# A fused retention and gated feed-forward kernel: loading the first weight slice ahead of the second pair's q and v, and splitting the first block of x in two

## The chip, the cores and the metric

The kernel runs on one core of a Trainium2 chip. The metric is the device time of one execution in microseconds (us); smaller is better. Engines are named as in the profile: PE is TensorE's matmul, PEld its weight load, DVE VectorE, ACT ScalarE, POOL GpSimd, SP SyncE.

## What is computed

There are 4 sequences of 768 tokens with 8 heads of 64 channels. The first half of the work is a retention recurrence, the second a feed-forward block with a sigmoid gate over all 3072 tokens, with a model width of 512 and a hidden width of 1536:

```python
# retention: q, k, v are [4, 8, 768, 64]; gamma = 1 - 2 ** (-5 - h)
for t in range(S):
    state = gamma * state + k[t] outer v[t]
    y[t] = scale * (q[t] @ state)
# feed-forward: x is y with the heads side by side, [3072, 512]
out = (sigmoid(x @ w_gate) * (x @ w_val)) @ w_out
```

## The kernel before

**Retention in chunks.** The recurrence is worked off in 24 chunks of 128 tokens. A chunk needs the transposes of k and q (PE, then a copy out of the accumulator by ACT or DVE), the scores of k against q (PE), a causal mask on them (DVE), the product of q with the state so far (`inter`), the product of the masked scores with v (`intra`), the chunk's own addition to the state (`state`, summed by DVE and cast by ACT), and a multiplication by a decay table that leaves the chunk's 128 columns of x (`y_out`, DVE). The first four chunks have versions of their own, whose names end in `_run`: chunks 0 and 1 are the first pair, 2 and 3 the second, and each pair's k, q and v come in one load (`kr`, `qr`, `vr`, line 75). `scale_run` (line 265) multiplies v by a table, and both `state_run` and `intra_run` need its result.

**Feed-forward in blocks of 512 tokens.** There are six such blocks, t = 0 to 5. An "up" (`up`, line 364) is one of the 12 slices of 128 hidden channels, n1: four matmuls with `wg`, four with `wv`, a sigmoid on ACT and a product on DVE that writes `hT`. `up_columns` (line 378) does the same for two values of n1 on 256 of the 512 tokens. A "down" multiplies `hT` by `wo` for 128 tokens and writes rows of the output. The first block of x is made by the first four chunks, so that its ups can begin only when `y_out_run` has delivered columns.

**Order.** The order of the instructions of each engine is the order in which the Python text issues them; nothing is rearranged. Each engine works its own list in order and waits on semaphores where an operand comes from another engine. Lines 435 to 508 write the start out by hand; after that, a table `plan` says behind which up or down of a block a step of the retention is put. Loads that convert to bf16, and most others, are issued by POOL one after the other (lines 98 to 109, 437, 445, 451, 452, 480 to 487), so POOL's own operations stand in the same list as its loads. Before the change, that list is: k of the first pair, q of the first pair, k, q and v of the second pair, a mask, gate and value slice 0, another mask, slices 1 and 2, the second `scale_run`, a decay table, slices 3 to 5, two more tables, four slices of `wo`, and the chunks from 4 on. A gate and value slice s (line 84) serves the ups n1 = 2s and 2s + 1.

**Identity products.** `keep_on(n)` (line 411) issues n matmuls of the identity with itself whose result nobody reads. They stand in PE's list at five places of the start, 29, 5, 9, 10 and 24 of them, each 128 columns wide.

The start of PE's list is, in order: 29 identity products; transposes of k, `state_run(0)`; 5 identity products; transposes of q; 9 identity products; `scores_run(0)`; transposes of the second pair's k; `inter_run`; transposes of the second pair's q; `intra_run(0)`; 10 identity products; `scores_run(1)`; `inter_run(2)`; 24 identity products; `state_run(1)`; up n1 = 0 on the first 256 tokens; `inter_run(3)`; `intra_run(1)`; ups 1 to 3 on the first 256 tokens; ups 0 to 3 on the second 256 tokens; then ups 4 to 11 on 512 tokens each.

Of the kernel before, what the change touches and what calls it, by code (L numbers as in the profile page):

```python
# [9 lines left out]
F32 = mybir.dt.float32  # L10
BF16 = mybir.dt.bfloat16
I32 = mybir.dt.int32
AX = mybir.ActivationFunctionType
ALU = mybir.AluOpType
# [3 lines left out]
def kernel(  # L18
# [10 lines left out]
    nc = tc.nc  # L29
# [3 lines left out]
    C = 128  # L33
# [41 lines left out]
    def load_run(x, a, dtype, eng, name):  # L75
        t = const.tile([128, H, 2 * D], dtype, name=name, tag=name, bufs=1)
        eng.dma_start(out=t, in_=x[0, :, a * 2 * C:(a + 1) * 2 * C, :].rearrange("h (p j) d -> p h (j d)", j=2))
        return t
# [5 lines left out]
    def load_gate_val(s):  # L84
        cols = slice(s * 256, (s + 1) * 256)
        for dst, w in ((wg, moe_w_gate), (wv, moe_w_val)):
            nc.gpsimd.dma_start(out=dst[:, :, cols],  # L87
                                in_=w.rearrange("(kk p) n -> p kk n", p=128)[:, :, cols])
# [9 lines left out]
    kr[0] = load_run(k, 0, BF16, nc.gpsimd, "kr0")  # L98
    ident = const.tile([128, 128], BF16, name="ident")
    make_identity(nc, ident)  # L100
    tokr = const.tile([128, 2, 2], I32, name="tokr")
    nc.gpsimd.iota(tokr, pattern=[[2 * C, 2], [1, 2]], base=0, channel_multiplier=2)
    tokv = const.tile([128, NCH], I32, name="tokv")
# [2 lines left out]
    toky = const.tile([128, 384], I32, name="toky")  # L106
    nc.gpsimd.iota(toky, pattern=[[1, 384]], base=0, channel_multiplier=0)
    kr[1] = load_run(k, 1, BF16, nc.gpsimd, "kr1")
    qr[1] = load_run(q, 1, BF16, nc.gpsimd, "qr1")

    lgh = const.tile([128, H], F32, name="lgh")
    for h in range(H):
# [23 lines left out]
    def tab_y(c):  # L136
        first = c if c in taby else c - 1
        return taby[first][:, :, (c - first) * C:(c - first + 1) * C]

    def make_taby(c, pairs=range(NP)):  # L140
        n = taby[c].shape[2]
        for p in pairs:
            nc.scalar.activation(taby[c][:, p, :], toky[:, c * C:c * C + n], AX.Exp, scale=lgp[:, p:p + 1], bias=lsc)
# [8 lines left out]
    def bank(shape, dt=F32):  # L152
        return pf.tile(shape, dt, tag="ff", name="ff")
# [50 lines left out]
    def state_out(g, z):  # L204
        for i in range(2):
            half = slice(i * D, (i + 1) * D)
            nc.scalar.copy(zbd[g % 4][half, :, half], z[half])  # L207
# [20 lines left out]
    def intra(g):  # L228
        first = g % NCH == 0
        for p in range(NP):  # L230
            for i, st in enumerate((stA[g], stB[g])):
                nc.tensor.matmul(y[g][i * D:(i + 1) * D, p, :], vs[g][:, 2 * p + i, :], st[:, p, :],  # L232
                                 start=(first and p == 0), stop=True, skip_group_check=True)

    def y_out(g):
        c = g % NCH
        if g % 4 == 0:
            xT[g // 4] = at.tile([128, NP, 512], BF16, tag="xT", name="xT")
        col = (g % 4) * C
        nc.vector.tensor_tensor(xT[g // 4][:, :, col:col + C], y[g], tab_y(c), op=ALU.mult)  # L240


    kT, qT = {}, {}
# [21 lines left out]
    def scale_run(a, eng):  # L265
        vsr[a] = const.tile([128, H, 2, D], BF16, name=f"vsr{a}")
        eng.tensor_tensor(vsr[a], runs(vr[a]), tabr[:, a].unsqueeze(3).to_broadcast([128, H, 2, D]), op=ALU.mult)  # L267
# [54 lines left out]
        else:  # L322
            nc.vector.tensor_tensor(new_za(g), za[g - 1], zz[g], op=ALU.add)

    def y_out_run(g):
        if g == 0:
            xT[0] = at.tile([128, NP, 512], BF16, tag="xT", name="xT")
        cols = slice(g * C, (g + 1) * C)
        in_runs = "x n (p j) -> x n j p"
        nc.vector.tensor_tensor(xT[0][:, :, cols].rearrange(in_runs, j=2), y[g].rearrange("x n (j p) -> x n j p", j=2),  # L330
                                tab_y(g).rearrange(in_runs, j=2), op=ALU.mult)

    def step_t(g):
        transposes(g)
# [27 lines left out]
    hT = {}  # L362

    def up(t, n1, lo=0, hi=512):
        if t not in hT:
            hT[t] = ffn.tile([128, NFF, 512], BF16, tag="hT", name="hT", bufs=2)
        ps = []
        for w in (wg, wv):
            u = bank([128, 512])
            for kk in range(KT):  # L370
                nc.tensor.matmul(u[:, lo:hi], w[:, kk, n1 * 128:(n1 + 1) * 128], xT[t][:, kk, lo:hi],  # L371
                                 start=(kk == 0), stop=(kk == KT - 1))
            ps.append(u)
        gs = ffn.tile([128, 512], F32, tag="gs", name="gs")
        nc.scalar.activation(gs[:, lo:hi], ps[0][:, lo:hi], AX.Sigmoid)  # L375
        nc.vector.tensor_tensor(hT[t][:, n1, lo:hi], gs[:, lo:hi], ps[1][:, lo:hi], op=ALU.mult)  # L376

    def up_columns(t, n1s, lo, hi):
        n = hi - lo
        ps = []  # L380
        for w in (wg, wv):
            u = bank([128, 512])
            for i, n1 in enumerate(n1s):
                for kk in range(KT):
                    nc.tensor.matmul(u[:, i * n:(i + 1) * n], w[:, kk, n1 * 128:(n1 + 1) * 128], xT[t][:, kk, lo:hi],  # L385
                                     start=(kk == 0), stop=(kk == KT - 1))
            ps.append(u[:, :len(n1s) * n])
        gs = ffn.tile([128, 512], F32, tag="gs", name="gs")
        g = gs[:, :len(n1s) * n]
        nc.scalar.activation(g, ps[0], AX.Sigmoid)  # L390
        nc.vector.tensor_tensor(hT[t][:, n1s[0]:n1s[-1] + 1, lo:hi], g.rearrange("p (i n) -> p i n", n=n),  # L391
                                ps[1].rearrange("p (i n) -> p i n", n=n), op=ALU.mult)
# [15 lines left out]
        row = t * 512 + sm * 128  # L408
        nc.sync.dma_start(out=out[row:row + 128, :], in_=ob)

    def keep_on(n, u=None):
        if u is None:
            u = bank([128, 512])
        for _ in range(n):
            nc.tensor.matmul(u[:, :128], ident, ident, start=True, stop=True)  # L415

    def last_down(t):
        row = t * 512 + 384
# [15 lines left out]

    make_taby(0)
    scale_run(0, nc.vector)
    vr[1] = load_run(v, 1, F32, nc.gpsimd, "vr")
    maskr = const.tile([128, 2, 2, D], F32, name="maskr")
    nc.gpsimd.memset(maskr, 1.0)
    for i in range(2):  # L440
# [1 line left out]
        nc.gpsimd.affine_select(half, half, pattern=[[-1, 2], [1, 2], [2, D]], base=0, channel_multiplier=-2,  # L442
                                compare_op=ALU.is_ge, fill=0.0)
    maskr2 = maskr.rearrange("x j i p -> x (j i p)").unsqueeze(1).to_broadcast([128, 2, 4 * D])
    load_gate_val(0)
    causal = const.tile([128, 128], F32, name="causal")
    nc.gpsimd.memset(causal, 1.0)
    nc.gpsimd.affine_select(causal, causal, pattern=[[1, 128]], base=0, channel_multiplier=-1,
# [1 line left out]
    causal4 = causal.unsqueeze(1).to_broadcast([128, NP, 128])  # L450
    load_gate_val(1)
    load_gate_val(2)
    scale_run(1, nc.gpsimd)
    make_taby(2, range(2))
    warm = bank([128, 512])
    keep_on(29, warm)
    kT[0], qT[0], kT[1], qT[1] = (new_run_T() for _ in range(4))
    transpose_run(kr[0], kT[0], [nc.scalar])
    state_run(0)
    sum_run(0)  # L460
    sum_run(1)
    keep_on(5, warm)
    transpose_run(qr[0], qT[0], [nc.scalar, nc.vector])
    state_out(0, zz[0])
    state_out(1, za[1])
    keep_on(9, warm)
    scores_run(0)
    masks_run(0, 0)
    masks_run(0, 1)
    transpose_run(kr[1], kT[1], [nc.scalar])  # L470
    make_taby(2, range(2, 4))
    inter_run(0)
    inter_run(1)
    transpose_run(qr[1], qT[1], [nc.scalar])
    nc.scalar.preload_act_table(AX.Sigmoid)
    intra_run(0)
    y_out_run(0)
    y_out_run(1)
    extend_taby(3)
    for s in range(3, NFF // 2):  # L480
        load_gate_val(s)
# [3 lines left out]
        load_out(s)  # L485
    for g in range(4, 8):
        load_chunk(g)
    keep_on(10)
    scores_run(1)
    masks_run(1, 0)  # L490
    inter_run(2)
    keep_on(24)
    state_run(1)
    sum_run(2)
    state_out(2, za[2])
    masks_run(1, 1)
    sum_run(3)
    up(0, 0, 0, 256)
    inter_run(3)
    intra_run(1)  # L500
    y_out_run(2)
    y_out_run(3)
    up(0, 1, 0, 256)
    state_out(3, za[3])
    up(0, 2, 0, 256)
    up(0, 3, 0, 256)
    up_columns(0, range(0, 2), 256, 512)
    up_columns(0, range(2, 4), 256, 512)


    def ups(t):
# [2 lines left out]
    def downs(t):  # L514
        return [lambda sm=sm, i=i: down(t, sm, i) for sm in range(4) for i in range(2)]

    plan = {
        0: [(9, step_t, 4), (11, step_t, 5), (12, block, None, 4), (12, casts, 4), (13, step_t, 6), (14, block, 4, None)],
        1: [(0, step_t, 7), (2, block, None, 6), (3, step_t, 8), (4, casts, 6), (5, step_t, 9), (7, block, 6, 8),
            (9, casts, 8), (11, step_t, 10), (13, step_t, 11), (15, block, 8, 10), (17, casts, 10), (20, block, 10, None),  # L520
            (22, scale_v, 12), (23, scale_v, 13)],
# [7 lines left out]
    for t in range(NT):  # L529
        groups = ups(t) + downs(t)  # L530
        if t == NT - 1:
            groups[-2:] = [lambda: last_down(t)]
        if t == 0:
            groups = groups[4:]
            for g in range(8, 12):
                load_chunk(g)
        if t == 1:
            groups[:10] = [lambda n1=n1: up(1, n1, 0, 256) for n1 in range(10)]
            groups[10:10] = [lambda n1=n1: up_columns(1, range(n1, n1 + 2), 256, 512) for n1 in range(0, 10, 2)]
            for g in range(12, 16):  # L540
                load_chunk(g)
        if t == 2:
            load_chunk(18)
            load_chunk(19)
        if t == 3:
            load_chunk(22)
            load_chunk(23)
        for i, group in enumerate(groups):
            if i == len(groups) - 9:
                for g in range(4 * t + 8, 4 * t + 12):  # L550
                    if XBAR <= g < NG:
                        xbar(g)
            if t == 1 and i == len(groups) - 4:
                load_chunk(16)
                load_chunk(17)
            if t == 2 and i == len(groups) - 4:
                load_chunk(20)
                load_chunk(21)
            group()
            for at_group, step, *g in plan[t]:  # L560
                if at_group == i:
                    step(*g)
# [30 lines left out]
```

## Time and profile before

| | |
|---|---|
| median of 13 runs | 237.13 us |
| lowest and highest of them | 235.15 and 238.11 us |
| the execution that was profiled | 237.16 us |
| its span, in which the profile's times count | 235.5 us |
| PE busy | 224.4 us, 95% of the span |
| DVE, ACT, POOL busy | 118.3, 90.8, 77.2 us |
| moved by DMA | 27.05 MB |

The 13 runs fall in two groups: five lie between 235.15 and 235.76 us, eight between 236.92 and 238.11 us. The profiled execution belongs to the second group and is close to the median.

The profile is one execution. Its span runs from the first to the last instruction; the 1.66 us between span and time lie around it. A line of the timeline gives the start in us, the duration of the group in us, the engine, the line of the kernel, the operation, the result and its operands, shapes and the count; in square brackets stands for how long the engine was idle just before and what released it. "issue" there means that the profile shows no operand for which the engine waited. PEclk is the clock that was granted to PE, as a share of the full one.

### The profile page before, as it was taken

The page shows a single profiled execution, that of the slowest core. Times are in us where ns is not written, and L with a number is a line of the kernel's source. Part 1 is how long each engine was busy: PE and PEld are TensorE (multiplying, and loading weights), DVE is VectorE, ACT ScalarE, POOL GpSimd, SP SyncE. Part 2 cuts the span into 40 slices and gives each one's busy share as a digit, 9 for nine tenths or more (in the row PEclk, how much of TensorE's full clock was granted, in tenths as well). Part 3 has the DMA queues.
Part 4 walks back from the last instruction along what each step waited for, and adds up shares of the span by engine and source line. Part 5 has one row for each costly group of instructions (what it writes and reads, how often), then busy time and mean ns, then how long its engine had stood idle before and what let it go on. Part 6 is the DMA issues. An engine that isn't in the chain of part 4 may idle for free.

```text
span 235.5 us, 4687 instructions
## 1 busy us (share of the span) xinstructions
PE 224.4 (95%) x1904; PEld 128.2 (54%) x1925; DVE 118.3 (50%) x226; ACT 90.8 (39%) x167; POOL 77.2 (33%) x99
## 2 busy tenths in 40 slices
PE   4996999999999999999999999999999999999994
PEld 4773844456889745454545445445445454444444
DVE  5665343436887474185952546845256712234301
ACT  5953333344656421444340432621632421333211
POOL 7899856998852453426000000000000000000000
PEclk9997999999999999999999999999999999999999
DMA  8999999999999999989702253002200001200022
GB/s 138 218 185 196 200 206 210 220 235 246 230 152 101 154 171 229 202 142 161 89 0 90 93 109 70 0 0 92 90 0 3 0 32 66 85 0 0 1 92 89
DMA packets 73302, 27.05 MB, mean 115 GB/s; under 512 B 59840, under 2 KB 68928, under 8 KB 73280
## 3 DMA queue, kind: packets, MB, share of 16 engines
q0 software_dynamic: 55440, 16.78, 66.6%
q1 hardware_dynamic: 17696, 9.90, 17.8%
q8 instruction: 15, 0.25, 0.4%
q10 hardware_dynamic: 144, 0.07, 0.1%
q14 instruction: 7, 0.06, 0.1%
HBM read 28.31 MB, written 6.29 MB: 147 GB/s over the span
## 4 chain that ended last, share of the span: by engine, by line
PE 77%; DMA 10%; POOL 6%; DVE 2%; issue 2%; ACT 1%; DVEq 0%
PE ff L371 39%; PE ff L402 24%; DMA wv<-in_moe_w_val_dram 4%; DMA kn<-in_k_dram 4%; PE ff L385 4%; PE ff L232 2%; PE ff L183 2%; DMA vr<-in_v_dram 2%; POOL wg L87 2%; POOL wv L87 2%; PE ff L195 2%; PE ff L162 1%; PE ff L423 1%; PE z L201 1%; POOL vsr L267 1%
## 5 line engine op out<-in xcount | busy, mean ns | idle before, releaser
L376 DVE TENSOR_TENSOR hT<-gs,ff 128x512 bf16<-128x512 f32 (+1 forms) x72 | 45.2, 634 | 63.9 <-PE ff L371 58.9
L371 PE MATMUL ff<-xT,wg 128*128 128x512 bf16 (+1 forms) x277 | 68.1, 361 | 1.2 <-DVE xT L330 0.7
L371 PE MATMUL ff<-xT,wv 128*128 128x512 bf16 (+1 forms) x287 | 68.5, 362 | 0.1
L375 ACT ACTIVATE gs<-ff 128x512 f32<-128x512 f32 (+1 forms) x72 | 39.9, 556 | 71.8 <-PE ff L371 64.7
L402 PE MATMUL ff<-wo,hT 128*128 128x512 bf16 x267 | 61.1, 379 | 0.9 <-issue 0.5
L371 PEld LDWEIGHTS <-wv 128*128 128x128 bf16 x288 | 28.6, 99 | 28.5
L402 PEld LDWEIGHTS <-hT 128*128 128x128 bf16 x276 | 26.3, 98 | 31.2 <-DVE hT L376 0.6
L371 PEld LDWEIGHTS <-wg 128*128 128x128 bf16 x288 | 27.4, 99 | 28.3 <-issue 0.8
L407 ACT COPY ob<-ff 128x512 f32<-128x512 f32 x23 | 13.5, 586 | 49.1 <-PE ff L402 40.2
L62 POOL DMA_DIRECT2D vf<-in_v_dram x20 | 18.3, 917 | 17.5 <-DVE vs L174 10.5
L240 DVE TENSOR_TENSOR xT<-ff,taby 128x512 bf16<-128x512 f32 x20 | 12.9, 686 | 21.0 <-PE ff L232 21.0
L67 POOL DMA_DIRECT2D kn<-in_k_dram x20 | 18.1, 905 | 13.4 <-DMA qkX<-kn 7.3
L207 ACT CAST zbd<-za 64x256 bf16<-64x256 f32 x38 | 15.3, 403 | 11.0 <-DVE za L219 8.0
L68 POOL DMA_DIRECT2D qn<-in_q_dram x20 | 18.2, 908 | 1.9 <-DMA wo<-in_moe_w_out_dram 1.6
L188 DVE TENSOR_TENSOR stA<-ff,causal 128x512 bf16<-128x512 f32 x20 | 13.6, 681 | 0.0
L189 DVE TENSOR_TENSOR stB<-ff,causal 128x512 bf16<-128x512 f32 x20 | 13.6, 681 | 0.0
L174 DVE TENSOR_TENSOR vs<-vf,tabv 128x512 bf16<-128x512 f32 x20 | 13.4, 684 | 0.0
L415 PE MATMUL ff<-ident 128*128 128x128 bf16 x77 | 6.6, 255 | 3.0 <-POOL ident masks.py:199 3.0
L164 ACT ACTIVATE qkT<-ff 128x1024 bf16<-128x1024 bf16 x8 | 8.2, 1026 | 1.6 <-PE ff L162 1.6
L391 DVE TENSOR_TENSOR hT<-gs,ff 128x512 bf16<-128x512 f32 x7 | 4.7, 687 | 5.5 <-PE ff L385 4.3
L415 PEld LDWEIGHTS <-ident 128*128 128x128 bf16 x77 | 5.7, 117 | 3.2 <-POOL ident masks.py:199 3.0
L385 PE MATMUL ff<-xT,wg 128*128 128x256 bf16 x56 | 7.3, 273 | 0.0
(85 smaller groups left out, 159.4 us busy)
## 6 DMA issues: line engine op xcount, KB each, us to landing
out_dram<-ob SPq DMA_DIRECT2D x23, 256.0 KB, 2.2
vf<-in_v_dram POOLq DMA_DIRECT2D x20, 256.0 KB, 6.8
kn<-in_k_dram POOLq DMA_DIRECT2D x20, 128.0 KB, 7.2
qn<-in_q_dram POOLq DMA_DIRECT2D x20, 128.0 KB, 7.6
wg<-in_moe_w_gate_dram POOLq DMA_DIRECT2D x6, 256.0 KB, 7.3
wv<-in_moe_w_val_dram POOLq DMA_DIRECT2D x6, 256.0 KB, 7.8
wo<-in_moe_w_out_dram POOLq DMA_DIRECT2D x4, 384.0 KB, 10.6
vr<-in_v_dram SPq DMA_DIRECT2D x1, 512.0 KB, 4.3
```

The source lines that it names most:

```text
L62: nc.gpsimd.dma_start(out=vf[g], in_=src(v, g))
L67: nc.gpsimd.dma_start(out=kn[g], in_=src(k, g))
L68: nc.gpsimd.dma_start(out=qn[g], in_=src(q, g))
L188: nc.vector.tensor_tensor(stA[g], sc[g][0], causal4, op=ALU.mult)
L189: nc.vector.tensor_tensor(stB[g], sc[g][1], causal4, op=ALU.mult)
L207: nc.scalar.copy(zbd[g % 4][half, :, half], z[half])
L371: nc.tensor.matmul(u[:, lo:hi], w[:, kk, n1 * 128:(n1 + 1) * 128], xT[t][:, kk, lo:hi], start=(kk == 0), stop=(kk == KT - 1))
L375: nc.scalar.activation(gs[:, lo:hi], ps[0][:, lo:hi], AX.Sigmoid)
L376: nc.vector.tensor_tensor(hT[t][:, n1, lo:hi], gs[:, lo:hi], ps[1][:, lo:hi], op=ALU.mult)
L385: nc.tensor.matmul(u[:, i * n:(i + 1) * n], w[:, kk, n1 * 128:(n1 + 1) * 128], xT[t][:, kk, lo:hi], start=(kk == 0), stop=(kk == KT - 1))
L402: nc.tensor.matmul(o, hT[t][:, n1, sm * 128:(sm + 1) * 128], wo[:, n1, :], start=(n1 == 0), stop=(n1 == NFF - 1))
L407: nc.scalar.copy(ob, o)
```

## The change

- Gate and value slice 0 takes the place of the second pair's q in POOL's list. The second pair's v and q come behind the first mask, v before q.
- The scaling of the second pair's v moves from POOL to DVE, behind the first pair's `y_out_run`.
- A block of x is held as two parts of 256 tokens, `[128, 2, NP, 256]`, instead of `[128, NP, 512]`. The first pair's `y_out_run` is done in halves: first channels 0 to 255 of both chunks, then the rest.
- Identity products are 512 columns wide (the identity is read four times over) and are 8, 2, 2, 4 and 2 in number. They all write the tile `warm`.
- The second pair's q is transposed behind the first ups instead of before `intra_run(0)`, and its copy is shared by ACT and DVE.
- Ups 0 to 5 (not 0 to 3) are done on 256 tokens at a time with `up_columns`. The first two come right behind the first pair, in two rows: the products with channels 0 to 255 of x, then the rest. Ups 2 and 3 on the first part stand between `inter_run(2)` and `inter_run(3)`, ups 4 and 5 behind `intra_run(1)`; the second part follows for all six. The table `plan` for block 0 is shifted by two, so each of its steps stands behind the same up or down as before.
- `state_run(1)` comes before `scores_run(1)`, and `sum_run(3)` between the two calls of `masks_run(1, ...)`. The load of the sigmoid's table on ACT comes before the first `inter_run`.

The core of the diff:

```diff
     kr[1] = load_run(k, 1, BF16, nc.gpsimd, "kr1")
-    qr[1] = load_run(q, 1, BF16, nc.gpsimd, "qr1")
+    load_gate_val(0)
...
-            xT[g // 4] = at.tile([128, NP, 512], BF16, tag="xT", name="xT")
+            xT[g // 4] = new_xT()
...
-    def up_columns(t, n1s, lo, hi):
+    def up_columns(t, n1s, lo, hi, rows=1):
         n = hi - lo
-        ps = []
-        for w in (wg, wv):
-            u = bank([128, 512])
-            for i, n1 in enumerate(n1s):
-                for kk in range(KT):
-                    nc.tensor.matmul(u[:, i * n:(i + 1) * n], w[:, kk, n1 * 128:(n1 + 1) * 128], xT[t][:, kk, lo:hi],
-                                     start=(kk == 0), stop=(kk == KT - 1))
+        us = [bank([128, 512]), bank([128, 512])]
+        for row in range(rows):
+            for w, u in zip((wg, wv), us):
+                for i, n1 in enumerate(n1s):
+                    for kk in range(row * KT // rows, (row + 1) * KT // rows):
+                        nc.tensor.matmul(u[:, i * n:(i + 1) * n], w[:, kk, n1 * 128:(n1 + 1) * 128],
+                                         x_cols(t, kk, lo, hi), start=(kk == 0 and (rows == 1 or i == 0)),
+                                         stop=(kk == KT - 1), skip_group_check=rows > 1)
...
-            nc.tensor.matmul(u[:, :128], ident, ident, start=True, stop=True)
+            nc.tensor.matmul(u, ident, ident4, start=True, stop=True)
...
-    vr[1] = load_run(v, 1, F32, nc.gpsimd, "vr")
     maskr = const.tile([128, 2, 2, D], F32, name="maskr")
...
-    load_gate_val(0)
+    vr[1] = load_run(v, 1, F32, nc.gpsimd, "vr")
+    qr[1] = load_run(q, 1, BF16, nc.gpsimd, "qr1")
...
-    scale_run(1, nc.gpsimd)
...
-    transpose_run(qr[1], qT[1], [nc.scalar])
-    nc.scalar.preload_act_table(AX.Sigmoid)
+    keep_on(4, warm)
     intra_run(0)
-    y_out_run(0)
-    y_out_run(1)
+    for n in range(2):
+        for g in range(2):
+            y_out_run(g, n)
...
-    keep_on(10)
-    scores_run(1)
-    masks_run(1, 0)
-    inter_run(2)
-    keep_on(24)
+    keep_on(2, warm)
+    scale_run(1, nc.vector)
+    up_columns(0, range(0, 2), 0, 256, 2)
+    transpose_run(qr[1], qT[1], [nc.scalar, nc.vector])
     state_run(1)
     sum_run(2)
     state_out(2, za[2])
+    scores_run(1)
+    masks_run(1, 0)
+    sum_run(3)
     masks_run(1, 1)
-    sum_run(3)
-    up(0, 0, 0, 256)
+    inter_run(2)
+    up_columns(0, range(2, 4), 0, 256)
     inter_run(3)
     intra_run(1)
     y_out_run(2)
     y_out_run(3)
-    up(0, 1, 0, 256)
     state_out(3, za[3])
-    up(0, 2, 0, 256)
-    up(0, 3, 0, 256)
-    up_columns(0, range(0, 2), 256, 512)
-    up_columns(0, range(2, 4), 256, 512)
+    up_columns(0, range(4, 6), 0, 256)
+    for n1 in range(0, 6, 2):
+        up_columns(0, range(n1, n1 + 2), 256, 512)
...
-            groups = groups[4:]
+            groups = groups[6:]
```

More of the change, by code (lines that the diff above doesn't have):

```diff
@@ L100 @@
     make_identity(nc, ident)
+    ident4 = ident.unsqueeze(1).to_broadcast([128, 4, 128])
     tokr = const.tile([128, 2, 2], I32, name="tokr")
@@ L233, in intra, with new_xT, x_cols @@
                                  start=(first and p == 0), stop=True, skip_group_check=True)
+    def new_xT():
+        return at.tile([128, 2, NP, 256], BF16, tag="xT", name="xT")
+    def x_cols(t, kk, lo, hi):
+        if hi - lo == 512:
+            return xT[t][:, :, kk, :]
+        half = lo // 256
+        return xT[t][:, half, kk, lo - half * 256:hi - half * 256]
     def y_out(g):
@@ L237, in y_out @@
         if g % 4 == 0:
-            xT[g // 4] = at.tile([128, NP, 512], BF16, tag="xT", name="xT")
-        col = (g % 4) * C
-        nc.vector.tensor_tensor(xT[g // 4][:, :, col:col + C], y[g], tab_y(c), op=ALU.mult)
+            xT[g // 4] = new_xT()
+        col = (g % 2) * C
+        nc.vector.tensor_tensor(xT[g // 4][:, g % 4 // 2, :, col:col + C], y[g], tab_y(c), op=ALU.mult)
     kT, qT = {}, {}
@@ L323, in sum_run, with y_out_run @@
             nc.vector.tensor_tensor(new_za(g), za[g - 1], zz[g], op=ALU.add)
[L325 to L328, printed above, removed]
+    def y_out_run(g, n=None):
+        if 0 not in xT:
+            xT[0] = new_xT()
+        cols = slice(g % 2 * C, (g % 2 + 1) * C)
+        of = slice(0, NP) if n is None else slice(2 * n, 2 * n + 2)
         in_runs = "x n (p j) -> x n j p"
-        nc.vector.tensor_tensor(xT[0][:, :, cols].rearrange(in_runs, j=2), y[g].rearrange("x n (j p) -> x n j p", j=2),
-                                tab_y(g).rearrange(in_runs, j=2), op=ALU.mult)
+        nc.vector.tensor_tensor(xT[0][:, g // 2, of, cols].rearrange(in_runs, j=2),
+                                y[g][:, of].rearrange("x n (j p) -> x n j p", j=2),
+                                tab_y(g)[:, of].rearrange(in_runs, j=2), op=ALU.mult)
     def step_t(g):
@@ L370, in up @@
             for kk in range(KT):
-                nc.tensor.matmul(u[:, lo:hi], w[:, kk, n1 * 128:(n1 + 1) * 128], xT[t][:, kk, lo:hi],
+                nc.tensor.matmul(u[:, lo:hi], w[:, kk, n1 * 128:(n1 + 1) * 128], x_cols(t, kk, lo, hi),
                                  start=(kk == 0), stop=(kk == KT - 1))
@@ L376, in up @@
         nc.vector.tensor_tensor(hT[t][:, n1, lo:hi], gs[:, lo:hi], ps[1][:, lo:hi], op=ALU.mult)
-    def up_columns(t, n1s, lo, hi):
+    def up_columns(t, n1s, lo, hi, rows=1):
+        if t not in hT:
+            hT[t] = ffn.tile([128, NFF, 512], BF16, tag="hT", name="hT", bufs=2)
         n = hi - lo
-        ps = []
-        for w in (wg, wv):
-            u = bank([128, 512])
-            for i, n1 in enumerate(n1s):
-                for kk in range(KT):
-                    nc.tensor.matmul(u[:, i * n:(i + 1) * n], w[:, kk, n1 * 128:(n1 + 1) * 128], xT[t][:, kk, lo:hi],
-                                     start=(kk == 0), stop=(kk == KT - 1))
-            ps.append(u[:, :len(n1s) * n])
+        us = [bank([128, 512]), bank([128, 512])]
[6 more added lines that the diff above has]
+                                         stop=(kk == KT - 1), skip_group_check=rows > 1)
+        ps = [u[:, :len(n1s) * n] for u in us]
         gs = ffn.tile([128, 512], F32, tag="gs", name="gs")
@@ L409, in down, with keep_on @@
         nc.sync.dma_start(out=out[row:row + 128, :], in_=ob)
-    def keep_on(n, u=None):
-        if u is None:
-            u = bank([128, 512])
+    def keep_on(n, u):
         for _ in range(n):
-            nc.tensor.matmul(u[:, :128], ident, ident, start=True, stop=True)
+            nc.tensor.matmul(u, ident, ident4, start=True, stop=True)
     def last_down(t):
@@ L452 @@
     load_gate_val(2)
-    scale_run(1, nc.gpsimd)
     make_taby(2, range(2))
-    warm = bank([128, 512])
-    keep_on(29, warm)
+    warm = bank([128, 4, 128])
+    keep_on(8, warm)
     kT[0], qT[0], kT[1], qT[1] = (new_run_T() for _ in range(4))
@@ L461 @@
     sum_run(1)
-    keep_on(5, warm)
+    keep_on(2, warm)
     transpose_run(qr[0], qT[0], [nc.scalar, nc.vector])
@@ L465 @@
     state_out(1, za[1])
-    keep_on(9, warm)
+    keep_on(2, warm)
     scores_run(0)
@@ L471 @@
     make_taby(2, range(2, 4))
+    nc.scalar.preload_act_table(AX.Sigmoid)
     inter_run(0)
     inter_run(1)
-    transpose_run(qr[1], qT[1], [nc.scalar])
-    nc.scalar.preload_act_table(AX.Sigmoid)
+    keep_on(4, warm)
     intra_run(0)
-    y_out_run(0)
-    y_out_run(1)
+    for n in range(2):
+        for g in range(2):
+            y_out_run(g, n)
     extend_taby(3)
@@ L487 @@
         load_chunk(g)
-    keep_on(10)
-    scores_run(1)
-    masks_run(1, 0)
-    inter_run(2)
-    keep_on(24)
+    keep_on(2, warm)
+    scale_run(1, nc.vector)
+    up_columns(0, range(0, 2), 0, 256, 2)
+    transpose_run(qr[1], qT[1], [nc.scalar, nc.vector])
     state_run(1)
@@ L517 @@
     plan = {
-        0: [(9, step_t, 4), (11, step_t, 5), (12, block, None, 4), (12, casts, 4), (13, step_t, 6), (14, block, 4, None)],
+        0: [(7, step_t, 4), (9, step_t, 5), (10, block, None, 4), (10, casts, 4), (11, step_t, 6), (12, block, 4, None)],
         1: [(0, step_t, 7), (2, block, None, 6), (3, step_t, 8), (4, casts, 6), (5, step_t, 9), (7, block, 6, 8),
```

## Prediction

> **What bounds the kernel now.** The page gives PE 224.4 us busy in a span of 235.5, so I first asked PE's waits from 21 us to the end: they sum to 1.2 us. From there on the kernel is one unbroken line of matmuls, and only the start can give time. The timeline of PE over the start (us, duration, count, idle before):
>
> ```profile
> 13.77 0.30 PE L277 MATMUL ff<-qkT 64*64 64x128 bf16 x6 [0.23 <-ACT qkT L258]
> 14.22 0.58 PE L277 MATMUL ff<-qkT 64*64 64x128 bf16 x26 [0.15 <-issue]
> 14.97 1.50 PE L415 MATMUL ff<-ident 128*128 128x128 bf16 x24
> 16.78 0.61 PE L371 MATMUL ff<-xT,wg 128*128 128x256 bf16 x4
> ...
> 18.22 0.40 PE L293 MATMUL ff<-qkT,zbd 128*128 128x128 bf16 x4 [0.40 <-ACT zbd L207]
> ...
> 20.42 0.21 PE L302 MATMUL ff<-stA,vsr 64*64 64x128 bf16 x1 [1.24 <-issue]
> ...
> 20.59 0.28 PE L371 MATMUL ff<-xT,wg 128*128 128x256 bf16 x1
> 21.55 0.80 PE L371 MATMUL ff<-xT,wg 128*128 128x256 bf16 x3 [0.67 <-DVE xT L330]
> 22.14 1.06 PE L371 MATMUL ff<-xT,wv 128*128 128x256 bf16 x4
> ...
> 24.60 0.60 PE L371 MATMUL ff<-xT,wg 128*128 128x256 bf16 x4
> ...
> 32.42 1.03 PE L371 MATMUL ff<-xT,wg 128*128 128x512 bf16 x4
> ```
>
> Read four things. The first up (L371) begins at 16.78, though DVE has the first pair's x ready at 14.24; before it PE runs 24 identity products. `intra_run(1)` (L302) halts for 1.24 us with no operand missing. The second up halts for 0.67 us for `y_out_run(3)`, whose columns 256 to 511 it does not read: in the layout `[128, NP, 512]` the two ranges of addresses interleave. And from 22.14 four matmuls of 256 columns follow after 0.86 us, from 24.60 after 0.44. The last has its cause in the windows of 3.41 us that fit the granted clock (columns: PE, PEld, DVE, ACT, POOL busy and counts, then the clock):
>
> ```profile
> 10.83:14.25 3.42, 2.71 (x74) 2.02 (x73) 2.94 (x5) 3.32 (x5) 3.42 (x6) 1.00 1.22 204
> 14.25:17.66 3.41, 3.41 (x94) 2.99 (x93) 2.06 (x4) 1.08 (x2) 3.41 (x4) 1.00 1.44 193
> 17.66:21.07 3.41, 1.58 (x39) 0.92 (x38) 2.54 (x6) 0.88 (x3) 3.41 (x5) 1.00 1.45 196
> 21.07:24.49 3.42, 2.94 (x14) 2.01 (x14) 0.85 (x2) 1.58 (x4) 3.42 (x5) 0.50 1.46 199
> ```
>
> After a window with PE busy for 1.58 of 3.41 us, the next one ran at half clock, which costs half of it, 1.7 us; after 2.71 the clock stayed. The line is thus somewhere between.
>
> The Trainium skill ("TensorE: Matmul & The Clock Gate", Part 1) lets the clock fall after at least one idle window of about 3.4 us. By that rule the 1.24 us halt would cost no clock, and 1.7 us of the sum below would not be there to gain; the rows above show otherwise, and I go by them.
>
> The halt "for issue" I read from a count. In PE's program the matmul at 14.22 is instruction 448 and the one at 20.42 is instruction 704, 256 apart; the page has
>
> ```profile
> q8 instruction: 15, 0.25, 0.4%
> ```
>
> and 3,852 PE instructions over 15 packets are 257 each. So instructions arrive in blocks of 256. Instruction 192 ran at about 8.4 (the 14th transpose of q, from 8.07). A block is entered 8.4, 14.2, 20.4: taking it that a block is asked for when the one before it is entered, it comes 5.8 to 6.2 us later while the loads are running, and PE halts when it eats 256 instructions faster.
>
> The Trainium skill ("Runtime: NRT & Kernel Launch", Instruction fetch mechanics) has the same blocks of 256 and says that the cost of crossing one is mostly hidden. By that, fewer identity products would be worth nothing and the sum 1.24 us smaller; the row at 20.42 decides against it.
>
> **The change, walked through.** Both kernels do ups 0 to 5, then up 6 in full width. Before, up 6 begins at 32.42. The gain is 32.42 minus its start after.
>
> *To the first x.* Identity products cost 0.427 us for 512 columns at half clock (four times the 0.107 per 128 that the 24.60 and 22.14 rows give per column) and 0.215 at full. Eight from 2.97 end at 6.38; 29 narrow ones ended in time for k's landing at 6.22, and the transposes began at 6.27. That is 0.1 late; the next two wide ones (0.43) for five narrow (0.3) make it 0.2 late for the scores (9.40 to 9.6). The four masks on DVE end at 12.6 instead of 12.41, `intra_run(0)` at 13.1 instead of 12.88. `y_out_run` in four halves: the 512-element operation took 0.68; a 256-element one (the sum L323) 0.42, half of 0.68 is 0.34. I take 0.36 and get the first halves at 13.8, all at 14.5.
>
> *Slice 0.* POOL's loads and their landings, by the view of DMA asked around each issue: first pair's k 1.32 to 6.2, q 3.04 to 7.6, second k 4.39 to 9.8, second q 5.28 to 11.5, v 6.72 to 13.0, slice 0 `wg` 8.85 to 14.45, `wv` to 16.0, slice 1 to 17.3 and 18.7, slice 2 to 20.6 and 21.95. They land in order. Slice 0 moves up past q and v; each of its halves takes 1.4 to 1.6, so it lands at 11.2 and 12.8 (by issue plus its own 5.6 and 6.4: 10.9 and 12.4), ahead of 13.8. The bytes in front of slice 1 are the same, so slices 1 and 2 stay at their times. v and q are issued at about 8.05 and 8.9 (the mask of 1.25 us stands before them) and land at 14.3 and 16.0.
>
> *Ups 0 and 1, first part.* 16 matmuls of 256 columns at 0.11 are 1.75; in two rows, from 13.85 to 15.6. Scaling v on DVE (1.23 by the first pair's row, against 1.95 on POOL) runs 14.5 to 15.75 beside it. Queued behind it on DVE are the product for `hT` and half of q's copy; neither is wanted before 16.
>
> *Second pair.* PE's transposes of q wait for the landing: 16.0, not 15.6. They end at 16.45 and `state_run(1)` at 16.85. ACT copies its half by 17.25 (0.60), DVE its own by 17.7, behind the 0.69 of the product. Scores 17.3 to 18.15. DVE: sum to 18.1, masks to 19.3, sum to 19.65, masks to 20.85. PE covers that with `inter_run(2)` and ups 2 and 3 (18.4 to 20.15; `wv` slice 1, 18.7, is wanted at 19.3), then `inter_run(3)`; the last half of `intra_run(1)` waits for the mask and ends at 21.15. Ups 4 and 5: 21.15 to 22.9, and `wv` slice 2 (21.95) is wanted at 22.0. `y_out_run(2)` and `(3)` end at 22.85 on DVE, just in time. The second part of six ups is 3 x 1.75 = 5.25, to **28.15**.
>
> *Cross-check.* From 13.1 the work is 10.4 of ups, 2.8 of the second pair (rows L253, L314, L277, L293, L302), 0.43 of identity products: 26.7. The other 1.45 are idle: 0.5 for x, 0.4 for q, 0.45 for its copy, 0.1 or so for a mask. Bounds of these waits: nothing (up 6 at 26.7) and twice as much (29.6).
>
> *Instruction blocks.* After, instruction 192 falls in `scores_run(0)` (about 10.1), so 448 arrives at 15.9 to 16.3; it is the last part of `state_run(1)`, 16.8. Instruction 704 is wanted at 24.8 and there by 23.0. No halt; the first margin is only 0.5, and a miss would cost as much as it is late.
>
> *Clock.* The window 14.25 to 17.66 would have PE busy for some 2.6 of 3.41 us, next to the 2.71 that kept the clock. Nothing is charged.
>
> *Sum.* 32.42 - 28.15 = 4.27: 1.24 halt, 0.67 false wait and 1.7 clock go (3.6), and some 0.7 more from ups where identity products and waiting stood. Later loads cover it: `wo` lands 32.1 to 37.4 and would be wanted from 38.5, the chunk after the first four at 38.7 and 39.6 against 41. Steps of later blocks stand behind the same ups as before. So 237.16 - 4.27 = **232.9**; the profiled execution stands at the median (237.13), so this is the forecast for the median too.
>
> **Rivals.**
> - *The clock still falls once.* Three short waits between 13.3 and 17.3 take the place of one long one; if a window catches them all, PE is busy for about 2.2 us, between 1.58 and 2.71, where the trace decides nothing. Price 1.7: **234.6**. Against it, the wide products and early ups fill PE before and after.
> - *The loads pace it.* The page's chain runs through a load of k that lands at 40.17 and hands over to PE L371. If that were a wait, an earlier start would gain nothing: **237.2**. Against it, L371 shows no idle time there.
> - *Slice 0 does not come early.* The loads in flight share the same engines; if moving up in the list does not move the landing and slice 0 lands with all that is in flight, at slice 1's 18.7, then PE, which works in order, holds the second pair's transposes behind the ups too. From 13.85 on each us late is a us lost: 4.85 late, 237.8, and an idle window from 13.3 to 18.7 costs half a window's clock as well: **239.5**, slower. Against it, all landings before are in order, 1.4 apart.
>
> **How the numbers follow.** The measurement tells about 0.5% from no change: 235.95 to 238.3. Chances: forecast 0.68, clock 0.17, loads pace 0.08, slice late 0.07. Faster 0.85, same 0.08, slower 0.07. The forecast's own range is 231.5 (all waits gone) to 234.4 (twice the waits). For 8 in 10 I go from 231.6 to 235.6, which takes in the clock case with a us of waits.
>
> **What would show it.** Right: no idle for "issue" over 0.3 us before 30; the first up at about 13.9; up 6 near 28.2; clock 1.00 from 7.5 on. Wrong: a window at 0.50, the first up later than 15, transposes of the second q later than 17, or new waits behind 40 us.

## The result and the profile after

| | before | after |
|---|---|---|
| median | 237.12 us (48 runs, 235.15 to 239.23) | 234.41 us (11 runs, 233.67 to 235.61) |
| profiled execution / its span | 237.16 / 235.5 us | 234.55 / 232.8 us |
| PE busy | 224.4 us | 222.7 us |

The ratio is 0.9901 with a 95% interval of 0.9874 to 0.9928: faster by 1.0%, 2.7 us in the medians. The forecast was 232.9 with a range of 231.6 to 235.6. The direction and the range held; the gain was forecast 1.5 us too large.

First the start, in the timeline of PE (columns as before; L400 is `up_columns`, L264 a transpose, L288 scores, L384 an up of 512 tokens):

```profile
12.62 0.60 PE L429 MATMUL ff<-ident 128*128 128x512 bf16 x2
13.53 0.60 PE L400 MATMUL ff<-xT,wg 128*128 128x256 bf16 x4 [0.29 <-DVE xT L342]
...
14.83 0.60 PE L400 MATMUL ff<-xT,wv 128*128 128x256 bf16 x4
16.05 0.64 PE L264 MATMUL ff<-ident,qr 128*64 128x128 bf16 x16 [0.62 <-DMA qr<-in_q_dram]
17.38 0.88 PE L288 MATMUL ff<-qkT 64*64 64x128 bf16 x32 [0.31 <-ACT qkT L269]
...
21.23 1.05 PE L400 MATMUL ff<-xT,wg 128*128 128x256 bf16 x8
22.38 1.05 PE L400 MATMUL ff<-xT,wv 128*128 128x256 bf16 x8
...
28.50 1.03 PE L384 MATMUL ff<-xT,wg 128*128 128x512 bf16 x4
```

The first up begins at 13.53 instead of 16.78, the halt for "issue" and the false wait of the second up are gone, and up 6 begins at 28.50 instead of 32.42. That is 3.92 us. The windows that fit this execution's clock:

```profile
9.68:13.09 3.41, 3.38 (x74) 2.03 (x74) 2.88 (x6) 3.27 (x7) 3.29 (x7) 1.00 1.31 258
13.09:16.51 3.42, 2.51 (x33) 1.93 (x31) 2.87 (x6) 1.44 (x2) 3.42 (x5) 1.00 1.54 190
16.51:19.92 3.41, 3.06 (x90) 2.49 (x85) 2.56 (x6) 1.83 (x4) 2.61 (x5) 1.00 1.45 196
```

The window with the most waiting, 13.09 to 16.51, still has PE busy for 2.51 of 3.42 us, and the clock stays at 1.00.

Every matmul from up 6 to the last one runs 3.92 us earlier than before, to a hundredth. DVE's last copy shows it, first before, then after:

```profile
232.34 0.29 DVE L430 COPY ob<-ff 128x128 f32<-128x128 f32 x1 [0.91 <-PE ff L423]
```

```profile
228.42 0.29 DVE L444 COPY ob<-ff 128x128 f32<-128x128 f32 x1 [0.92 <-PE ff L437]
```

Yet the span is only 2.62 us shorter (to a hundredth, 235.46 before and 232.84 after). From the end of that copy to the end of the span, called the end stretch below, it was 235.46 - 232.63 = 2.83 us; now it is 232.84 - 228.71 = 4.13. **1.3 us are given back behind the last instruction that computes.** The view of DMA over the last microseconds says what is different. Before, from 231.3 on (size, us from issue to landing):

```profile
out_dram<-ob SPq DMA_DIRECT2D x1, 128.0 KB, 1.7
out_dram<-ob ACTq DMA_DIRECT2D x1, 64.0 KB, 1.7
out_dram<-ob SPq DMA_DIRECT2D x1, 64.0 KB, 1.6
```

After, from 227 on:

```profile
GB/s 46 300 382 328 37 0 341 269 89 194 9 127 164 27 23 23 23 20 2 0 0 0 0 0 0 0 0 0 0 0 0 0 0 0 0 0 0 0 0 0
...
q8 instruction: 1, 0.02, 0.6%
...
out_dram<-ob SPq DMA_DIRECT2D x1, 128.0 KB, 3.7
out_dram<-ob ACTq DMA_DIRECT2D x1, 64.0 KB, 3.4
out_dram<-ob SPq DMA_DIRECT2D x1, 64.0 KB, 2.9
```

All three last writes take 1.3 to 2 us longer, and a packet of q8, the queue of instructions, lies among them: it starts at 228.46 and takes 0.88 us for its 16 KB. At the end of the row of GB/s, the traffic runs on for a microsecond at 23 GB/s, about a sixteenth of the 300 to 380 at its start: what is left of the writes goes at the pace of one of 16 engines, as if the others were done and one had stood behind the packet. Before, the last packet of q8 came at 223.9 and met none of these writes.

### The profile page after: what moved, and what is told of

Its sections match the earlier page's. It is cut to its first block, busy times and chain, and to the rows that moved or that the text cites. A ratio compares the mean times of both kernels' runs of the same rounds, so it can differ in the third digit from the quotient of the medians.

```text
span 232.8 us, 4604 instructions
## 1 busy us (share of the span) xinstructions
PE 222.7 (96%) x1871; PEld 124.4 (53%) x1882; DVE 119.4 (51%) x228; ACT 90.0 (39%) x165; POOL 75.4 (32%) x98
## 3 DMA queue, kind: packets, MB, share of 16 engines
q0 software_dynamic: 55440, 16.78, 64.3%
## 4 chain that ended last, share of the span: by engine, by line
PE 84%; POOL 5%; DMA 4%; issue 2%; DVE 2%; ACT 1%; POOLq 0%
PE ff L384 43%; PE ff L418 25%; PE ff L400 6%; DMA wv<-in_moe_w_val_dram 4%; PE ff L233 2%; PE ff L184 2%; PE ff L196 2%; PE ff L163 1%; PE ff L437 1%; PE z L202 1%; POOL wg L87 1%; POOL kr L77 1%; POOL qr L77 1%; POOL wv L87 1%; DVE stA L189 1%
## 5 line engine op out<-in xcount | busy, mean ns | idle before, releaser
L389 DVE TENSOR_TENSOR hT<-gs,ff 128x512 bf16<-128x512 f32 (+1 forms) x66 | 42.1, 646 | 58.7 <-PE ff L384 53.8
L384 PE MATMUL ff<-xT,wg 128*128 128x512 bf16 (+1 forms) x264 | 63.6, 363 | 0.0
L384 PE MATMUL ff<-xT,wv 128*128 128x512 bf16 (+1 forms) x264 | 63.5, 363 | 0.0
L388 ACT ACTIVATE gs<-ff 128x512 f32<-128x512 f32 (+1 forms) x66 | 37.2, 565 | 64.7 <-PE ff L384 57.6
L384 PEld LDWEIGHTS <-wv 128*128 128x128 bf16 x264 | 25.8, 98 | 27.0
L384 PEld LDWEIGHTS <-wg 128*128 128x128 bf16 x264 | 24.9, 98 | 26.0 <-DVE xT L251 0.3
L400 PE MATMUL ff<-xT,wg 128*128 128x256 bf16 x88 | 11.6, 273 | 0.3 <-DVE xT L342 0.3
L400 PE MATMUL ff<-xT,wv 128*128 128x256 bf16 x88 | 11.6, 273 | 0.1
L407 DVE TENSOR_TENSOR hT<-gs,ff 128x512 bf16<-128x512 f32 x11 | 7.5, 686 | 7.1 <-PE ff L400 5.9
L406 ACT ACTIVATE gs<-ff 128x512 f32<-128x512 f32 x11 | 6.5, 598 | 7.5 <-PE ff L400 7.5
L400 PEld LDWEIGHTS <-wg 128*128 128x128 bf16 x88 | 8.4, 98 | 1.7 <-issue 0.6
```

## The experiments

My theory after the result: TensorE's program is 86 instructions shorter (3,766 instead of 3,852), so the last of its blocks of 256 is now fetched while the last rows are written. The rival: the late landing is chance, or comes from the writes themselves.

**The last fetch moved earlier.** 48 instructions more, in the same time:

```diff
-    keep_on(8, warm)
+    keep_narrow(32, warm)        # 128 columns each
```

> The changed kernel with its first eight wide identity products written as 32 narrow ones, which take the same time at half clock (8 x 0.427 against 32 x 0.107 us) and add 48 instructions to TensorE's program (3,766 to 3,814). Theory (tail): in the changed kernel the last block of TensorE's instructions is fetched at 228.5 us, among the last output writes, and the writes land 1.3 us late; with 48 more instructions the fetch comes some 4 us earlier. Expected: last stores land about 1.7 us after issue instead of 2.9 to 3.7, the time between the last copy and the end of the span back from 4.1 to 2.8 us, median 1.3 us below the changed kernel's 234.41, so 233.1. Rival (the late landing is chance or has to do with the writes themselves): end stretch as before or varying, median 234.4.

Median 233.55 us (6 runs, 233.25 to 234.54), ratio to the kernel before 0.9866 (0.9832 to 0.9899). In its profile up 6 begins at 28.53, as in the changed kernel (28.50), and the end stretch is 2.81 us. The last packet of q8 comes at 223.3. The last writes:

```profile
out_dram<-ob SPq DMA_DIRECT2D x1, 128.0 KB, 1.7
out_dram<-ob ACTq DMA_DIRECT2D x1, 64.0 KB, 1.7
out_dram<-ob SPq DMA_DIRECT2D x1, 64.0 KB, 1.6
```

The profiled execution took 233.25, 1.30 us less than that of the changed kernel, all of it at the end. The medians differ by 0.86 us, less than the 1.3 forecast. The traces show the end of the profiled executions alone; whether the late landing costs as much in every execution of the changed kernel is not shown.

**The last fetch removed.** All identity products but the first eight left out:

```diff
-    keep_on(2, warm)     # three times
-    keep_on(4, warm)
```

> The changed kernel without any identity products but the first eight: 20 instructions fewer (3,746). Theory (tail): the last block of instructions is entered only after the last matmul, or not at all, so its fetch no longer meets the last writes: end stretch 2.8 us, median 233.1, if the clock holds. On the clock: the windows of 3.4 us around 8 to 17 us lose up to 0.9 us of PE's busy time, down to some 2.2 to 2.4; if one of them then falls below what keeps the clock, a window at 0.50 shows and costs up to 1.7 us: 234.8. Rival (the end stretch has nothing to do with instruction blocks): end stretch 4.1 us, median 234.4 or, with the clock lost, 236.

Median 234.26 (6 runs, 233.35 to 235.8), ratio 0.9899 (0.9856 to 0.9943). Its trace has 14 packets of q8 instead of 15, and the end stretch is 2.82 us, as the theory has it. But the clock fell in the profiled execution, between 10.16 and 13.57:

```profile
6.74:10.16 3.42, 1.67 (x77) 1.41 (x77) 1.03 (x3) 2.37 (x5) 3.18 (x8) 1.00 1.61 178
10.16:13.57 3.41, 3.41 (x84) 2.62 (x75) 2.72 (x5) 2.62 (x6) 3.41 (x6) 0.50 1.32 262
```

There it cost little: ups 0 and 1 began a microsecond late, but the transposes behind them wait for q at 16 anyway, and up 6 began at 28.61. Over six runs, though, the times spread wider than those of the kernel above, three of them have a mean granted clock of 0.985 to 0.993, and the median shows no gain.

**The same kernel again:**

> The changed kernel once more, unaltered, so that its end stretch is seen in a second profile and its time beside the three others of this call. Theory (tail, tied to the instruction count): the last fetch of instructions again falls among the last writes, within about half a us, and the stretch from the last copy to the end of the span is again well above 2.8 us (3.3 to 4.1); median 234.4. Rival (chance): 2.8 us.

Median 234.36 (6 runs), ratio 0.9886 (0.9851 to 0.9921). In this second profile the last fetch starts at 227.1, again among the last writes; they take 2.7 to 3.5 us, and the end stretch is 3.9. Twice in two profiles, so chance is unlikely; two more profiles below show the same.

**The wide products alone, on the kernel before:**

```diff
-    keep_on(29, warm)
+    keep_wide(8, warm)           # 512 columns each
...
-    keep_on(10)
+    keep_wide(1, u); keep_on(5, u)
...
-    keep_on(24)
+    keep_wide(6)
```

> The kernel before with nothing changed but identity products made wide (29 narrow to 8 wide, 24 to 6, 10 to 1 wide and 5 narrow), so that TensorE's program has 3,766 instructions, as many as in the changed kernel. Theory: the halt of 1.24 us in intra_run(1) goes, because fewer than 256 instructions are eaten while the block is on its way, and the half clock with it (1.7 us); up 6 begins at about 29.5 instead of 32.42; and the last fetch falls among the last writes as in the changed kernel, so 1.3 us come back at the end: median 237.1 - 2.9 + 1.3 = 235.5. Rival 1 (halt not from instruction count): 237.1. Rival 2 (the late landing at the end is not from the instruction count): end stretch 2.8 us and median 234.2.

Median 236.42 (12 runs), ratio 0.9975 (0.9945 to 1.0005): of the 1.6 us expected the ratio leaves 0.6, and the interval reaches no change. The end is as forecast: last fetch at 230.7, end stretch 3.9 us, with nothing changed in the ups or the loads. The clock is too: it stayed at 1.00 in this profile, behind a window with PE busy for 1.97 us:

```profile
18.68:22.09 3.41, 1.97 (x45) 1.28 (x43) 3.36 (x7) 1.19 (x3) 3.41 (x5) 1.00 1.45 196
```

But up 6 begins at 31.73, only 0.7 earlier than before, and not at 29.5. In this execution the clock rose a microsecond later than in the profile before, and there are two waits:

```profile
16.28 0.21 PE L277 MATMUL ff<-qkT 64*64 64x128 bf16 x1 [0.89 <-issue]
...
22.27 0.49 PE L371 MATMUL ff<-xT,wg 128*128 128x256 bf16 x3 [1.22 <-DVE xT L330]
```

The halt did not go, it moved. With fewer instructions ahead of it, block 448 begins at the end of `scores_run(1)` and is wanted at 15.4, before it is there; and the false wait grew from 0.67 to 1.22. I had worked out the block at 704 alone. The rule that I took from the profile before (a block comes 5.8 to 6.2 us after the one before it is entered) gives the new halt, after the fact: instruction 192 now lies in `scores_run(0)`, which this execution ran at about 10.2, and 10.2 plus 5.8 to 6.2 is 16.0 to 16.4. The packets of q8 tie both halts to a fetch more closely. Before, one lasts from 18.03 to 18.98, and the halt ends at 20.42, 1.44 us behind it; here one lasts from 13.81 to 14.83, and the halt ends at 16.28, 1.45 us behind it.

**All identity products narrow, on the changed kernel:**

```diff
-    nc.tensor.matmul(u, ident, ident4, start=True, stop=True)       # 8, 2, 2, 4, 2 of them
+    nc.tensor.matmul(u[:, 0, :], ident, ident, start=True, stop=True)  # 32, 8, 8, 16, 8
```

> The changed kernel with every wide identity product as four narrow ones: 108 instructions more (3,874). Theory (blocks of 256, each about 6 us after the one before it was entered): instruction 192 now falls in the transposes of q at about 8.2, so 448 arrives near 14.2; it lies in the first row of ups 0 and 1, reached near 13.7: a halt of about half a us. It is swallowed by the wait for q's landing at 16.05. Instruction 704 lies in intra_run(1), near 20.7, and is there by 20.4. The last fetch lies well ahead of the last writes. So up 6 at 28.5, end stretch 2.8 us, median 233.5: the wide products are worth nothing in this kernel, and at the end they cost. Rival (they are what removed the halt): halt of over 1 us back, half clock with it, 235 or more.

Median 233.59 (6 runs, 233.26 to 233.78), ratio 0.9856 (0.9829 to 0.9883), so 0.8 us below the changed kernel. No halt appears at all; the half microsecond that I expected in ups 0 and 1 did not show, in an execution whose x came a microsecond later (first up at 14.57). The packet of q8 for block 448 ends at 12.48; with the 1.45 us seen above the block would be there at about 13.9 (an estimate), and instruction 448 runs at 14.9. The last fetch lies at 217.2, the end stretch is 2.8. The width of the products is thus not needed to remove the halt in this kernel, and it costs at the end. What is left is the order of the work around the block boundaries, which no run varied by itself.

**The order of the loads undone:**

```diff
-    load_gate_val(0)             # behind the second k
+    qr[1] = load_run(q, 1, ...)  # and v behind scale_run(0), slice 0 behind the mask, as before
```

> The changed kernel with the loads in the order of the kernel before (second pair's q and v ahead of slice 0). Theory (loads land in order, each at its turn): slice 0 lands at 14.5 and 16.0 us, q at 11.5; the first up's gate part begins near 14.5, its value part at 16.0, ups 0 and 1 end at 17.3 instead of 15.3, the transposes of q follow at 17.3 instead of 16.05, and all behind is 1.25 us later: up 6 at 29.75, median 235.7. Rival (the order of loads does not matter, since the second pair then has its data earlier): median 234.4.

Median 236.16 (12 runs, 234.48 to 237.3), ratio 0.997 (0.9937 to 1.0004). In the profile the first ups wait for slice 0:

```profile
14.61 0.61 PE L400 MATMUL ff<-xT,wg 128*128 128x256 bf16 x4 [1.07 <-DMA wg<-in_moe_w_gate_dram]
15.73 0.61 PE L400 MATMUL ff<-xT,wv 128*128 128x256 bf16 x4 [0.51 <-DMA wv<-in_moe_w_val_dram]
```

and up 6 begins at 29.33, 0.83 us later rather than 1.25, as the value half of slice 0 came some 0.3 us sooner than I had put it. The window with these waits:

```profile
12.98:16.40 3.42, 1.83 (x15) 0.97 (x14) 3.02 (x5) 1.25 (x1) 3.42 (x6) 1.00 1.41 186
```

It kept the clock with PE busy for 1.83 us. In 4 of the 12 executions the mean granted clock was 0.991 to 0.993, which is what one half-clock window of 3.41 us makes of 235 (the profile before had 0.993); these four took 236.8 to 237.3. The median of the other eight is 235.70. The order of the loads is thus worth 1.75 us in the medians: 0.45 of it goes with the clock, and 1.3 is left, of which the profile shows 0.83 as waiting. The profiled execution itself, the fastest of the twelve, took 234.48 and so no longer than that of the changed kernel (234.55): its last fetch comes at 229.07, its last writes land after 2.0 to 2.8 us, and its end stretch is 3.24 us instead of 4.13.

**One tile for x** (on the kernel with 3,814 instructions, 233.55):

```diff
-        return at.tile([128, 2, NP, 256], BF16, tag="xT", name="xT")
+        return at.tile([128, NP, 512], BF16, tag="xT", name="xT")
...                                  # and the indices that go with it
```

> The changed kernel with 32 narrow products in place of the first eight wide ones (which measured 233.55, last fetch out of the last writes), and x in one tile [128, 4, 512] again. Theory (false wait): ups 4 and 5 on the first part halt after one matmul until y_out_run(3) has written columns they do not read, at about 22.7 us instead of going on at 21.3; up 6 begins 1.3 us later, at 29.8; median 234.9. Rival (the layout is worth nothing where DVE keeps up): 233.55.

Median 234.80 (9 runs), ratio 0.9909 (0.9882 to 0.9937), 1.25 us more, and the fastest of the nine is slower than the slowest of the six with x in two parts. The false wait is back, behind one matmul of ups 4 and 5:

```profile
22.05 0.28 PE L397 MATMUL ff<-xT,wg 128*128 128x256 bf16 x1
23.55 0.92 PE L397 MATMUL ff<-xT,wg 128*128 128x256 bf16 x7 [1.21 <-DVE xT L339]
```

**Ups 0 and 1 later** (same base):

```diff
-    keep_on(2, warm)
+    keep_on(8, warm)
     scale_run(1, nc.vector)
-    up_columns(0, range(0, 2), 0, 256, 2)
...
     masks_run(1, 1)
+    up_columns(0, range(0, 2), 0, 256, 2)
     inter_run(2)
```

> The same base of 233.55, with ups 0 and 1 on the first part moved behind the second pair's scores and masks; six more wide identity products stand in their old place, so that PE is as busy. Theory (what the change gains is useful work in the place of identity products and waiting): 1.75 us of matmuls move from a stretch where PE would wait for q's landing (16.05) into one where it does not wait, less the 0.6 us that PE idles before intra_run(1) ends; up 6 begins 1.1 to 1.75 us later, median 234.7 to 235.3. Rival (the second pair's chain on DVE sets the pace, and PE has room there): up 6 at 28.5 to 28.8, median 233.6 to 233.9.

Median 235.03 (12 runs), ratio 0.9934 (0.9907 to 0.9961): 1.5 us more. Instead of the two ups PE does this:

```profile
13.64 1.90 PE L429 MATMUL ff<-ident 128*128 128x512 bf16 x8
16.61 0.64 PE L264 MATMUL ff<-ident,qr 128*64 128x128 bf16 x16 [1.07 <-DMA qr<-in_q_dram]
```

Up 6 begins at 30.36, 1.83 us later. The second pair's chain leaves PE no room to do the two ups later for nothing.

The 1.75, 1.25 and 1.5 us of these three runs are what each step is worth with the others in place; they overlap and can't be added up to the gain. The scaling of v on DVE, the first ups in two rows and the halves of `y_out_run` were not varied by themselves.

## Why the prediction was right in direction and 1.5 us too low

- **What bounds the kernel.** Right. 3.92 us gained by up 6 are still 3.92 us at the last matmul; no load and no engine took anything back in the 200 us between. The rival that the loads pace the kernel, and the chain of the page that suggested it, fall.
- **The walk to up 6.** Off by 0.35 (28.50 against 28.15). The landings were forecast at 11.2, 12.8, 14.3 and 16.0 for slice 0, v and q and measured at 11.3, 12.7, 14.5 and 16.0; the transposes of q began at 16.05, the scores at 17.38 (17.3), ups 4 and 5 at 21.23 (21.15). The term that was too small is the landing of value slice 2: 22.31 instead of 21.95, and PE, which wanted it at 22.1, waited 0.28 (the row at 22.38). x came 0.3 earlier than forecast, in an execution whose clock rose at 6.27 instead of 7.42; the landing of q swallowed that.
- **The halt.** Right that it goes. The runs do not support that fewer instructions remove it: with narrow products throughout it stays away, and with wide ones on the kernel before it only moves. That the halts are waits for a block of instructions holds up: both stand at a multiple of 256 from instruction 192 and end 1.44 and 1.45 us behind a packet of q8. The 5.8 to 6.2 us of the prediction fit these two halts and are no fixed delay. With narrow products throughout, instruction 192 runs at 9.1 and its successor block is there some 4.8 us later, by the estimate of 13.9 above; and late in the kernel before, when the loads are over, the last packet starts at 223.9, while instruction 3,776 runs only at 229.1. In the changed kernel instruction 448 ran at 16.8, as forecast, and its packet had ended at 14.12.
- **The clock.** Right: nothing was to be charged. In 43 executions of the kernel before that stand beside these runs, 15 kept a mean granted clock above 0.9945 and took 236.29 us in the median, 25 lay between 0.990 and 0.9945 and took 237.66, and 3 were lower. In 18 executions of the changed kernel none lies below 0.995. By this split the half window is worth about 1.4 us rather than 1.7, and most, not all, executions of before paid it. The rows now put the limit between 1.67 us busy of 3.42 (fell) and 1.83 (kept), with four of the twelve executions of that last kernel slower at a lower mean clock; my 2.2 for the worst case was on the safe side. The Trainium skill ("TensorE: Matmul & The Clock Gate", Part 1) has the clock fall after an idle window; here windows that were busy for 1.58 and 1.67 us were enough.
- **The sum.** This is the step that failed. "The gain is 32.42 minus its start after" takes it that the end of the kernel stays as it is. It did not: the end stretch grew by 1.30 us. The same count of instructions with which I explained the halt at the start says that the last block boundary lies at 704 + 12 x 256 = 3,776, inside the old program of 3,852 and just behind the new one of 3,766. I checked three boundaries at the start and not the last one. That a last block is still fetched with 3,766, around the end of the last matmul (the packet at 228.46, that end at 228.38; 227.07 and 228.06 in the second profile), and not with 3,746 (14 packets), is what the traces show; what asks for it behind the last matmul stays open. 0.35 and 1.30 make the 1.65 between forecast (232.9) and profile (234.55).
- **The range.** It held, with some luck. 234.41 lies nearer to the price of the clock rival (234.6) than to the forecast, and the room that was left for a half-clock window took up a cost at the end that no term of the sum has.
- **Slice 0 not coming early.** Ruled out by its landing, as the prediction said it would be seen.

The Trainium skill ("Runtime: NRT & Kernel Launch", Instruction fetch mechanics) calls the cost of crossing a block mostly hidden. For most of the 15 blocks the traces agree; the halts of 1.24 and 0.89 us at the start and the 1.3 us at the end are where it is not.

The kernel with 32 narrow products in front (233.55 us) and the one with narrow products throughout (233.59) are both faster than the two kernels compared here.

## What to carry to other kernels

Work that is pulled into a stretch where an engine only waits, or is only kept warm, gains its full length if that engine is busy without a break from there on; but check the layout for false waits, since a halt moves as easily as it goes. When a gain is read at one point of the kernel, follow it to the last landing: here a third of it was lost behind the last instruction. Whoever adds or removes many instructions shifts where their blocks are fetched, so the boundaries belong in the working, the last one too.

## What was not expected of the hardware

A fetch of instructions can hold up data: three writes of 64 to 128 KB that land in 1.6 to 1.7 us took 2.0 to 3.7 when one packet of 16 KB (0.88 to 1.76 us) fell among them, in all four profiles of three kernels with 3,766 instructions; in the profiles with 3,746, 3,814, 3,852 or 3,874 none fell among them, and they did not. That the writes stood behind it on one DMA engine is read from the 23 GB/s at the end and was not varied by itself. The moment at which the clock first rises differs from execution to execution (5.8 to 8.6 us in these profiles) and moves the first x by up to a microsecond; most of that is gone by up 6 (28.2 to 28.9 us), since q lands when it lands.
